# Scatters of a routed kernel issued one at a time behind attention steps, and one key stage moved ahead

## The chip, the cores and the metric

The kernel runs on one core of a Trainium2 chip. The metric is the device time of one execution in microseconds (us). The kernel before takes 1244.17 us as the median of 3 runs (1242.67 to 1245.28). The profiled execution is a run of its own and took 1242.59 us, with a span of 1240.8 us between the first and last instruction.

## The reference

Three layers are computed in float32, one after the other, over 4608 tokens of 512 values.

```python
q_s = np.exp(q - q.max(-1)); q_s /= q_s.sum(-1)          # (8 batches, 8 heads, 576, 64)
k_s = np.exp(k - k.max(2));  k_s /= k_s.sum(2)
x = q_s @ (k_s^T @ v)                                    # then (4608, 512)
e = argmax(x @ w_gate + modality_bias[modality_id])      # one of 8 experts per token
x = gate * (relu(x @ w1[e]) @ w2[e])
out = (((x @ m1) * (x @ m2)) @ w3) @ w_out
```

## The kernel before, in words

**Stages.** An opening of some 180 us computes the attention and the routing. Then come the expert slots (each one expert with up to 512 tokens that were sorted to it), and then the last layer's products. TensorE is fed in float32 pieces: each factor is split into a high and a low part, and three products are summed.

**The opening.** The 8 batches are worked in four pairs, c = 0 to 3. `keys(c)` (L292 on) takes the maximum of the keys over the sequence (VectorE, L302 to L305, `tr`, `mx`), turns it with TensorE (L311, L314, L319), copies the maximum to `kr` (ScalarE, L322), subtracts it on GpSimd in 12 pieces (L328; for c = 0 on VectorE) and takes the exponential on ScalarE (L329) in four pieces. The keys sit in `kt`, two buffers for four pairs: pairs 0 and 2 in `kt0`, pairs 1 and 3 in `kt1`. `kvs(c)` (L332 on) multiplies keys and values (L347, four groups of 72 short matmuls), normalises (L354 to L356) and makes the small matrices `bd` (L360, L363, L368, L371). `queries(n)` (L382, L383) prepares three columns of queries in `qs`. `attend(c, j)`, nine times per pair and here called a step and written (c, j), turns the queries (L397), takes the exponential (L400, `qT`), multiplies with `bd` (L410, 32 short matmuls), reads the result out (ScalarE L420 and L421, VectorE L422 and L423 into a row of `xt`), and after every second step SP stores the rows to `x_dram` (L427). `route(c)` (L436 on) finds each token's expert and its place in the sorted order (VectorE, with one exponential at L453 and a few matmuls at L461, L463). `scatters(c)` (L475) then issues nine indirect DMAs on GpSimd's queue, one for 128 tokens each (L434), which write a token's number and gate, 8 bytes, to its place in `order_dram`. Ahead of each but the first stands a small memset of `nop` (L433).

**What sets the order.** Nothing is issued in program order. `Plan` records each operation with its engine, an assumed cost, the keys that it reads and writes, and a priority; `order()` then lists them, taking on each engine the ready operation with the smallest number (place in the program plus priority). Each engine runs its own list in that order, and waits are on semaphores. A scatter has priority +120, so that it stands behind what is recorded up to 120 places after it.

**After the opening.** `early_table()` (called for c = 2) makes a table of the first expert slots from the counts of pairs 0 and 1. For slot 0 SP reads the table (L608), loads the expert's first weights (`w1r`, L644, 2 MB), and then the token list `ord` (L637), which waits for the 18 scatters of pairs 0 and 1. GpSimd gathers the tokens (L655, four indirect DMAs). ScalarE casts `w1r` (L623, eight pieces) and scales the tokens (L659); VectorE and GpSimd take the low parts (L625); TensorE turns the tokens (L675); ScalarE and VectorE split them (L679, L680); then TensorE runs the first layer (L692) and the second (L712). The buffers of the expert stage are handed over from those of the attention at "Mb", after the last step.

The main loop of the opening is this:

```python
    for c in range(4):
        load("k", c + 2)
        keys(c + 1)
        if c:
            route(c - 1)
            if c < 3:
                scatters(c - 1)
        ...
        for j in range(NT):
            attend(c, j)
            if j % 3 == 2:
                queries(3 * c + j // 3 + 2)
        load("q", c + 2)
        kvs(c + 1)
        load("v", c + 2)
```

Of the kernel before, what the change touches and what calls it, by code (L numbers as in the profile page):

```python
# [21 lines left out]
NT = 9  # L22
# [10 lines left out]
BT = 768  # L33
HB = BT // 2
PAIRS = ((0, 0), (0, 1), (1, 0))
WHY = "the tables hold counts of the 4608 tokens only"


# [81 lines left out]
def K(*a):  # L120
    return a
# [21 lines left out]
def body(tc, q, k, v, mod, wgate, mbias, w1, w2, m1, m2, w3, wo, out):  # L143
    nc = tc.nc
    V, G, SC, PE, SP = nc.vector, nc.gpsimd, nc.scalar, nc.tensor, nc.sync
    P = Plan()
# [116 lines left out]
    def load(n, c):  # L263

        if c >= 4:
            return
        src, t = dict(k=(k, kt), q=(q, qt), v=(v, vt))[n]
        z = c % 2
        for i in range(2):
            dst = t[z][:, 4 * i : 4 * i + 4].rearrange("p g j d -> p g (j d)")  # L270
            fn = lambda dst=dst, i=i: SP.dma_start(dst, src[2 * c + i].rearrange("(g y) (r j) d -> (y r) g (j d)", y=2, j=NT))
            P.add("D", 3.7, fn, w=[K(n, z, g) for g in (2 * i, 2 * i + 1)], slack=1.0)
# [100 lines left out]
    def queries(n):  # L373

        if n >= 12:
            return
        c, g = n // 3, n % 3
        z = c % 2
        q_, x = qt[z], qx[z]
        kq = [K("q", z, g) for g in range(4)]  # L380
        js = slice(3 * g, 3 * g + 3)
        P.add("V", vt_(1536), lambda: V.tensor_reduce(x[:, :, js], q_[:, :, js], axis=AX.X, op=ALU.max), r=kq, w=[K("qx", z, g)])  # L382
        P.add("V", vt_(1536), lambda: V.tensor_tensor(qs[(3 * c + g) % 2].rearrange("p j h d -> p h j d"), q_[:, :, js], x[:, :, js].unsqueeze(3).to_broadcast([128, H, 3, D]), op=ALU.subtract), r=kq + [K("qx", z, g)], w=[K("qs", (3 * c + g) % 2)])  # L383
# [47 lines left out]
    def scatter(dst, src):  # L431
        if scattered[0]:
            G.memset(nop, 0.0)  # L433
        i = G.indirect_dma_start(out=order_dram, out_offset=bass.IndirectOffsetOnAxis(ap=dst, axis=0), in_=src, in_offset=None).ins  # L434
        tc.declare_no_dep(i, group="order", reason="every token has a row of its own")
        tc.add_to_no_dep_group("order", i)  # L436
        scattered[0] = True
# [34 lines left out]
        vv(lambda: V.tensor_scalar(s, s, 1e-9, None, op0=ALU.add), w=["s"])  # L472
        vv(lambda: V.reciprocal(tid[:, c, :, 1].bitcast(F32), s), r=["s"], w=[K("gate", c)])

    def scatters(c, after=()):  # L475
        for t in range(NT):
            P.add("G", (1.3, 0.1), lambda t=t: scatter(pi_[c % 2][:, t : t + 1], tid[:, c, t]), r=[K("pi", c % 2), K("gate", c), "order", *after], w=[K("scat", NT * c + t)], pri=120)


    tab = const.tile([1, 4, X0 + NX], I32, name="tab")  # L480
# [306 lines left out]
    biases()  # L787
    for c in range(4):
        load("k", c + 2)
        keys(c + 1)  # L790
        if c:
            route(c - 1)
            if c < 3:
                scatters(c - 1)
        if 2 * c == BEARLY:
            tpri[0] = -150
            early_table()
        if c == 3:
            fa_keys = [k_ for k_ in P.last if isinstance(k_, tuple) and k_[0] in ("k", "v") and k_[1] == 0] + ["mods", K("mods", 0), K("mods", 1), K("bias", 1), "bs", "bsb", "mod", "modf", "zer"]
            P.add("X", 0.0, to_experts_a, w=fa_keys + ["Ma"])  # L800
        for j in range(NT):
            attend(c, j)
            if j % 3 == 2:
                queries(3 * c + j // 3 + 2)
        load("q", c + 2)
        kvs(c + 1)
        load("v", c + 2)
    fb_keys = [k_ for k_ in P.last if isinstance(k_, tuple) and (k_[0] in ("q", "qs", "qx", "qT", "bd", "bdg", "mx", "kr", "cm", "rk", "kT", "vp") or k_[0] in ("k", "v") and k_[1] == 1)]
    P.add("X", 0.0, to_experts_b, w=fb_keys + ["tr4", "wg", "Mb"] + [K("bk", i) for i in (0, 1, 2, 3, 6, 7)])
# [346 lines left out]
```

## Time and profile before

| | us |
|---|---|
| median of 3 runs | 1244.17 |
| lowest and highest | 1242.67, 1245.28 |
| the profiled execution, its own time | 1242.59 |
| its span | 1240.8 |
| TensorE busy | 1147.5 (92%) |
| VectorE busy | 738.3 (59%) |
| ScalarE busy | 488.5 (39%) |
| GpSimd busy | 442.6 (36%) |

PE is TensorE's matmuls, PEld its weight loads, DVE is VectorE, ACT ScalarE, POOL GpSimd, SP the queue that issues most DMAs. A row of the timeline gives the start, the duration, the engine, the line, the operation, and in brackets the idle time before it and what ended it. "issue" is time in which the engine waited for nothing that the profile shows.

### The profile page before, as it was taken

The numbers are of one execution on the slowest core, as the hardware profiler recorded it, in microseconds if no ns is written. First come the engines' busy times: TensorE is split into PE (matmuls) and PEld (weight loads), VectorE is DVE, ScalarE is ACT, GpSimd is POOL, SyncE is SP. The second block draws the span as 40 slices with busy tenths as digits, with TensorE's granted clock in tenths as the row PEclk, the third lists the DMA queues.
The fourth block names the chain that finished last, engine by engine and source line by source line (L and its number), as shares of the span: only waits on it lengthen the run. The fifth ranks groups of instructions, "written<-read, shape, count | busy, mean of one in ns | idle before, by whom it ended". The sixth has DMA issues, their size and how long they took to land.

```text
span 1240.8 us, 20445 instructions
## 1 busy us (share of the span) xinstructions
PE 1147.5 (92%) x7939; PEld 1010.7 (81%) x7939; DVE 738.3 (59%) x1253; ACT 488.5 (39%) x907; POOL 442.6 (36%) x414
## 2 busy tenths in 40 slices
PE   4777559999989999999999999999999999999996
PEld 3565437888878888888987999999999998888885
DVE  7977678789258878778674745546473555213110
ACT  3544355445335444443463342324232434233220
POOL 0445638545033334323161434333343332111111
PEclk9867779999999999999999999999999999999998
DMA  9971166765236555445664222213131326534211
GB/s 354 391 296 62 61 226 149 272 203 167 81 117 209 162 188 189 164 165 179 222 191 131 86 77 103 79 74 103 51 103 56 139 86 244 197 111 171 101 44 41
DMA packets 84076, 187.52 MB, mean 151 GB/s; under 512 B 13022, under 2 KB 19714, under 8 KB 83970
## 3 DMA queue, kind: packets, MB, share of 16 engines
q1 hardware_dynamic: 76898, 166.68, 39.5%
q0 software_dynamic: 7072, 19.44, 4.6%
q8 instruction: 64, 1.05, 0.4%
q14 instruction: 42, 0.34, 0.1%
HBM read 142.25 MB, written 60.67 MB: 164 GB/s over the span
## 4 chain that ended last, share of the span: by engine, by line
PE 68%; DVE 2%; issue 1%; ACT 0%; DMA 0%; POOLq 0%; ACTq 0%; DVEq 0%
PE pb L1038 28%; PE pb L1114 15%; PE pb L712 12%; PE pb L692 10%; PE pb L931 2%; DVE ar L965 2%; PE pb L675 1%; PE pb L918 0%; DMA out_dram<-ca,oall 0%; DVE tt L907 0%; DVE al L907 0%; POOLq L1152 0%; ACT al L906 0%; DVE thm L907 0%; DVE ca L1014 0%
## 5 line engine op out<-in xcount | busy, mean ns | idle before, releaser
L1038 PE MATMUL pb<-al,ar 128*128 128x384 f32 x1728 | 307.8, 335 | 1.1 <-ACT sx L1044 0.8
L1038 PEld LDWEIGHTS pb<-al,ar 128*128 128x128 f32 x1728 | 300.0, 188 | 1.6 <-ACT sx L1044 1.1
L712 PE MATMUL pb<-ar 128*128 128x512 f32 (+1 forms) x960 | 214.1, 381 | 0.0
L692 PE MATMUL pb<-ar 128*128 128x512 f32 (+1 forms) x960 | 211.4, 380 | 0.0
L692 PEld LDWEIGHTS pb<-ar 128*128 128x128 f32 x960 | 173.6, 189 | 33.9 <-DVE ar L680 0.4
L712 PEld LDWEIGHTS pb<-ar 128*128 128x128 f32 x960 | 173.0, 189 | 32.9
L1114 PE MATMUL pb<-ar 128*128 128x512 f32 x864 | 196.0, 389 | 0.0
L1114 PEld LDWEIGHTS pb<-ar 128*128 128x128 f32 x864 | 162.2, 188 | 33.6
L907 DVE TENSOR_TENSOR ar<-ca,ar 128x512 fp32r<-128x512 f32 x80 | 54.9, 707 | 111.3 <-ACT ar L906 111.2
L1119 POOL DMA_INDIRECT out_dram<-ca,oall x36 | 35.6, 990 | 162.0 <-ACT ca L1117 139.2
L696 ACT ACTIVATE ar<-pb 128x512 fp32r<-128x512 f32 (+1 forms) x80 | 46.2, 578 | 117.9 <-PE pb L692 117.8
L1044 ACT COPY sx<-pb 128x384 f32<-128x384 f32 x96 | 46.1, 481 | 98.8 <-PE pb L1038 98.6
L742 POOL TENSOR_TENSOR ca<-ca 128x512 f32<-128x512 f32 x40 | 55.4, 1391 | 77.8 <-DVE ca L741 74.6
L697 DVE SCALAR_TENSOR_TENSOR ar<-pb,ar 128x512 fp32r<-128x512 f32 (+1 forms) x80 | 52.4, 656 | 42.9 <-ACT ar L696 40.6
L1117 ACT COPY ca<-pb 128x512 f32<-128x512 f32 x36 | 21.1, 585 | 131.2 <-PE pb L1114 101.3
L328 POOL TENSOR_TENSOR kt<-kt,kr 128x384 f32<-128x384 f32 x36 | 45.2, 1291 | 72.1 <-ACT kr L322 60.4
L625 DVE TENSOR_TENSOR ar<-w2r,ar 128x512 fp32r<-128x512 f32 x60 | 46.2, 796 | 37.6 <-ACT ar L623 36.6
L1047 POOL TENSOR_TENSOR ca<-ca,sx 128x384 f32<-128x384 f32 x24 | 27.0, 1124 | 113.9 <-ACT sx L1044 113.9
L1047 POOL TENSOR_TENSOR sx<-sx 128x384 f32<-128x384 f32 x24 | 28.7, 1195 | 104.9 <-ACT sx L1044 104.9
L715 ACT COPY yo<-pb 128x512 f32<-128x512 f32 (+1 forms) x40 | 22.6, 565 | 108.6 <-PE pb L712 96.9
L625 POOL TENSOR_TENSOR ar<-w2r,ar 128x512 fp32r<-128x512 f32 x20 | 31.1, 1554 | 85.7 <-ACT ar L623 85.7
L1044 ACT COPY ca<-pb 128x384 f32<-128x384 f32 x48 | 23.0, 479 | 92.2 <-PE pb L1038 82.6
(248 smaller groups left out, 1675.8 us busy)
## 6 DMA issues: line engine op xcount, KB each, us to landing
w1r<-in_moe_w_dram SPq DMA_DIRECT2D x10, 2048.0 KB
w2r<-in_moe_w_dram SPq DMA_DIRECT2D x10, 2048.0 KB
p_dram<-ca SPq DMA_DIRECT2D x48, 384.0 KB
ca<-p_dram SPq DMA_DIRECT2D x18, 1024.0 KB
ca<-in_moe_w_dram SPq DMA_DIRECT2D x32, 512.0 KB
kt<-in_k_dram SPq DMA_DIRECT2D x8, 1152.0 KB
qt<-in_q_dram SPq DMA_DIRECT2D x8, 1152.0 KB
vt<-in_v_dram SPq DMA_DIRECT2D x8, 1152.0 KB
```

What stands on the lines that cost most here:

```text
L328: P.add(en, c_ / 3 + 0.05, lambda hs=hs, e_=e_, js=js: e_.tensor_tensor(k_[:, hs, js], k_[:, hs, js], r_[:, hs].unsqueeze(2).to_broadcast( ...
L625: P.add(g, c, lambda: e.tensor_tensor(lo(), raw(), hi().bitcast(F32), op=ALU.subtract), r=[K(nm + "r", i), K(nm + "h", i), extra], w=[K(nm ...
L692: PE.matmul(p(), lhsT=W1(i)[:, TURN[kk], ms], rhs=XT(z)[:, kk, cols], start=(kk == 0 and c == 0), stop=(kk == 3 and c == 2))
L696: P.add("S", ps_(N), lambda hh=hh, p=p: SC.activation(hh(), p(), AF.Relu), r=[K("bk", pb), "Mb"], w=[K("hh", h, m) for h in hs])
L697: P.add("V", vt_(N), lambda hh=hh, hl=hl, p=p: V.scalar_tensor_tensor(out=hl(), in0=p(), scalar=0.0, in1=hh().bitcast(F32), op0=ALU.max, o ...
L712: PE.matmul(p(), lhsT=W2(i)[:, f, ns], rhs=HT(y)[:, f, cols], start=(f == 0 and c == 0), stop=(f == 7 and c == 2))
L742: P.add("G", gt_(512), lambda: G.tensor_tensor(Tf, Tf, Qf, op=ALU.add), r=[K("Q", b)], w=[K("T", b)])
L907: P.add("V", vt_(n), lambda: V.tensor_tensor(lo(), src, hi().bitcast(F32), op=ALU.subtract), r=list(sk) + [hk], w=[lk])
L1038: PE.matmul(bk(j), lhsT=Mt[:, f, a, i, m, t], rhs=X(y, x)[:, t], start=(fresh and t == 0 and n == 0), stop=(t == 1 and n == 2), skip_group ...
L1044: P.add("S", ps_(HB), lambda j=j, to=to: SC.copy(S(to), bk(j)), r=[bkk(j)], w=[sk(to)])
L1047: P.add("G", gt_(HB), lambda: G.tensor_tensor(S(1), S(1), S(2), op=ALU.add), r=[sk(2)], w=[sk(1)])
L1114: PE.matmul(bank[z], lhsT=PB(u % 2, i, f)[:, ts], rhs=WP(y, f), start=(f == 0 and n == 0), stop=(f == 7 and n == 2))
```

## The change

The two calls of `scatters` for pairs 0 and 1 become a list, `drops`. A scatter is taken from the list and recorded behind a step, and now reads that step's row of `xt` too; its priority is -900 instead of +120. Of the 18, four stand behind steps (1, 5) to (1, 8), nine behind (2, 0) to (2, 8), two behind a preparation of queries (after (2, 5) and (2, 8)), two behind the two halves of `bd` for pair 3, and one behind (3, 0). The scatters of pairs 2 and 3 stay as they were. `keys(3)` is recorded after step (1, 4); before, it was recorded at the start of c = 2. Lines up to 475 move down by one, those of the expert slots by ten.

```diff
+DROP = ((1, 5), (1, 6), (1, 7), (1, 8), (2, 0), (2, 1), (2, 2), (2, 3), (2, 4), (2, 5), (2, 6), (2, 7), (2, 8), (3, 0))
...
-    def scatters(c, after=()):
-        for t in range(NT):
-            P.add("G", (1.3, 0.1), lambda t=t: scatter(pi_[c % 2][:, t : t + 1], tid[:, c, t]), r=[K("pi", c % 2), K("gate", c), "order", *after], w=[K("scat", NT * c + t)], pri=120)
+    def scatters(c, after=(), ts=range(NT), pri=120):
+        for t in ts:
+            P.add("G", (1.3, 0.1), lambda t=t: scatter(pi_[c % 2][:, t : t + 1], tid[:, c, t]), r=[K("pi", c % 2), K("gate", c), "order", *after], w=[K("scat", NT * c + t)], pri=pri)
+
+    drops = []
+
+    def drip(*keys):
+
+        for key in keys:
+            if drops:
+                c, t = drops.pop(0)
+                scatters(c, [key], [t], -900)
...
     for c in range(4):
         load("k", c + 2)
-        keys(c + 1)
+        if c < 2:
+            keys(c + 1)
         if c:
             route(c - 1)
             if c < 3:
-                scatters(c - 1)
+                drops.extend((c - 1, t) for t in range(NT))
...
         for j in range(NT):
             attend(c, j)
+            if (c, j) == (1, 4):
+                keys(3)
+            if (c, j) in DROP:
+                drip(K("xt", (j // 2 + 5 * c) % 5, j % 2))
             if j % 3 == 2:
                 queries(3 * c + j // 3 + 2)
+                if (c, j) in ((2, 5), (2, 8)):
+                    drip(K("qs", (3 * c + j // 3 + 2) % 2))
         load("q", c + 2)
         kvs(c + 1)
+        if c == 2:
+            drip(*[K("bd", 2 + y) for y in range(2)])
         load("v", c + 2)
```

The planner turns this into other lists. First, GpSimd, from the subtraction of pair 2's keys (`kt_119`) on. `pi_106` holds the places of pair 0's tokens, `pi_107` those of pair 1; `kt_120` are pair 3's keys. Before, at the end of the first run of nine scatters:

```order
L434 DMA order_dram<-tid,pi_106 37376x2
L433 MEMSET nop 128x1
L434 DMA order_dram<-tid,pi_106 37376x2
L328 TENSOR_TENSOR kt_120<-kt_120,kr_147 128x2x192 x12
L433 MEMSET nop 128x1
L434 DMA order_dram<-tid,pi_107 37376x2
```

The same place in the change, from pair 2's subtraction on:

```order
L329 TENSOR_TENSOR kt_119<-kt_119,kr_146 128x2x192 x12
L435 DMA order_dram<-tid,pi_106 37376x2
L434 MEMSET nop 128x1
L435 DMA order_dram<-tid,pi_106 37376x2
L434 MEMSET nop 128x1
L435 DMA order_dram<-tid,pi_106 37376x2
L329 TENSOR_TENSOR kt_120<-kt_120,kr_147 128x2x192
L434 MEMSET nop 128x1
L435 DMA order_dram<-tid,pi_106 37376x2
L329 TENSOR_TENSOR kt_120<-kt_120,kr_147 128x2x192 x11
L434 MEMSET nop 128x1
L435 DMA order_dram<-tid,pi_106 37376x2
```

Before, nine scatters stood together ahead of pair 3's subtraction and nine together behind it. Now four stand ahead of its greater part, and the other 14 behind it, each with a wait for its step.

Second, ScalarE where pair 2's steps open: `bd_154` and `bd_155` are the small matrices that those steps read, `pp_82` their first result, `kt_120` pair 3's keys. In the change:

```order
L364 COPY kTs_158<-pb_75 64x512
L330 ACTIVATE kt_120<-kt_120 128x1152
L372 COPY bd_154<-pb_75 128x4x8
L364 COPY kTs_159<-pb_76 64x512
L454 ACTIVATE ca<-ca 128x72
L330 ACTIVATE kt_120<-kt_120 128x1152
L372 COPY bd_155<-pb_76 128x4x8
L330 ACTIVATE kt_120<-kt_120 128x1152
L421 ACTIVATE ca<-pp_82,eps 128x8
```

Before, the exponentials of `kt_120` stood far behind, among pair 2's last steps. Now three of the four stand here, and the read of the first result is behind all of them.

Third, ScalarE at the first expert slot, after the last step: `w1r` are the weights, `ord_94` the gates of slot 0's tokens, L453 (L454) the exponential of pair 3's routing. Before:

```order
L623 CAST ar<-w1r 128x512 x7
L659 ACTIVATE ca<-ca,ord_94 128x512
L623 CAST ar<-w1r 128x512
L659 ACTIVATE ca<-ca,ord_94 128x512 x2
L679 CAST ar<-pb_76 128x2x256
L659 ACTIVATE ca<-ca,ord_94 128x512
L679 CAST ar<-pb_78 128x2x256
L453 ACTIVATE ca<-ca 128x72
L679 CAST ar<-pb_76 128x2x256
```

In the change:

```order
L633 CAST ar<-w1r 128x512 x8
L669 ACTIVATE ca<-ca,ord_94 128x512 x2
L454 ACTIVATE ca<-ca 128x72
L669 ACTIVATE ca<-ca,ord_94 128x512 x2
L689 CAST ar<-pb_76 128x2x256
L689 CAST ar<-pb_78 128x2x256
```

The routing's exponential now stands ahead of two of the four scalings and of all casts of the turned tokens. On SP, the table reads and slot 0's `w1r` load stand between the stores of pair 2's rows now, where they stood behind all of them.

## Rows read from the trace of the kernel before

**Rows 1.** The page: busy time, share of the span and instructions of each engine.

```profile
PE 1147.5 (92%) x7939; PEld 1010.7 (81%) x7939; DVE 738.3 (59%) x1253; ACT 488.5 (39%) x907; POOL 442.6 (36%) x414
```

**Rows 2.** Timeline of PE: first expert matmuls, and the one later gap.

```profile
185.37 22.25 PE L692 MATMUL pb<-ar 128*128 128x512 f32 x93
...
351.49 1.94 PE L675 MATMUL pb<-ident,ca 128*128 128x128 f32 x8 [4.32 <-DVEq L836]
```

**Rows 3.** Windows of 4 us: stretch, length, busy us per engine (instructions), clock, DMA share, GB/s.

```profile
142.00:146.00 4.00, 0.53 (x2) 0.36 (x2) 0.00 (x0) 0.00 (x0) 3.08 (x5) 0.50 0.06 15
```

**Rows 4.** Timeline of PE, 91 to 152 us: start, duration, line.

```profile
91.44 1.25 PE L410 MATMUL pp<-bd,qT 64*64 64x73 f32 x64
...
97.88 1.11 PE L410 MATMUL pp<-bd,qT 64*64 64x73 f32 x38
...
107.03 0.65 PE L360 MATMUL pb<-ident,bd 128*64 128x128 f32 x2
...
128.76 2.37 PE L347 MATMUL pb<-vp,kt 64*64 64x65 f32 x144
...
135.60 1.20 PE L347 MATMUL pb<-vp,kt 64*64 64x65 f32 x44
...
148.31 2.88 PE L347 MATMUL pb<-vp,kt 64*64 64x65 f32 x92 [1.14 <-issue]
```

**Rows 5.** Timeline of POOL, 78 to 146 us.

```profile
78.61 15.70 POOL L328 TENSOR_TENSOR kt<-kt,kr 128x384 f32<-128x384 f32 x12 [18.45 <-ACT kr L322]
94.48 1.40 POOL L434 DMA_INDIRECT order_dram<-tid,pi  x1 [0.17 <-POOL kt L328]
...
105.69 0.96 POOL L434 DMA_INDIRECT order_dram<-tid,pi  x1 [0.19 <-issue]
118.41 14.62 POOL L328 TENSOR_TENSOR kt<-kt,kr 128x384 f32<-128x384 f32 x12 [11.76 <-DVE ca L422]
...
133.20 0.99 POOL L434 DMA_INDIRECT order_dram<-tid,pi  x1
...
144.49 0.97 POOL L434 DMA_INDIRECT order_dram<-tid,pi  x1 [0.19 <-issue]
```

**Rows 6.** DMA queues (packets, MB, share): whole run; then 94-95, 98-99, 168-169 us.

```profile
q8 instruction: 64, 1.05, 0.4%
...
q8 instruction: 1, 0.02, 5.9%
...
q8 instruction: 1, 0.02, 16.9%
...
q8 instruction: 1, 0.02, 5.5%
```

**Rows 7.** Timeline at the gathers: POOL's first, and PE's last piece of pair 3.

```profile
165.40 0.98 POOL L655 DMA_INDIRECT ca<-x_dram,ord  x1 [19.93 <-DMA x_dram<-ca]
...
171.02 0.56 PE L410 MATMUL pp<-bd,qT 64*64 64x73 f32 x9 [1.07 <-issue]
```

**Rows 8.** Timeline, 91 to 157 us: ACT's exponential; ACT, DVE, PE where pairs 2 and 3 open.

```profile
91.85 1.17 ACT L329 ACTIVATE kt<-kt 128x1152 f32<-128x1152 f32 x1
...
114.46 0.28 ACT L420 ACTIVATE ca<-pp,eps 128x8 f32<-128x8 f32 x1 [2.06 <-PE pp L410]
...
151.04 0.16 DVE L354 TENSOR_SCALAR rk<-pb 128x4 f32<-128x4 f32 x1 [11.43 <-PE pb L347]
...
155.68 1.09 PE L410 MATMUL pp<-bd,qT 64*64 64x73 f32 x32
```

**Rows 9.** Timeline after the last step, 172 to 186 us: DVE and ACT.

```profile
172.76 0.69 DVE L423 TENSOR_TENSOR ca<-pp,ca 128x512 f32<-128x512 f32 x1 [0.20 <-DVE ca L422]
...
176.65 1.34 ACT L659 ACTIVATE ca<-ca,ord 128x512 f32<-128x512 f32 x2
...
182.16 0.26 ACT L453 ACTIVATE ca<-ca 128x72 f32<-128x72 f32 x1 [2.12 <-DVE ca L452]
...
182.85 1.28 DVE L680 TENSOR_TENSOR ar<-pb,ar 128x512 fp32r<-128x512 f32 x2
```

## The prediction, made before the change was run

> **What bounds the kernel now.** I read the page, the timeline of TensorE, the windows of the opening, and then the queues. TensorE is busy for 92% of the span [rows 1]. From the first expert matmul at 185.37 us it streams almost without a gap; the one that stands out later (4.32 us, where the program branches) follows TensorE's own work [rows 2]. So the end moves with the start of the expert stage, nearly one for one, and what counts is how soon the opening ends. The reader should see in the windows of the opening a stretch in which VectorE and ScalarE do nothing at all (0.00 busy), TensorE executes 2 matmuls in 4 us, and its granted clock is 0.50 (the 1.2 GHz level) [rows 3]. Only GpSimd is busy there, with scatters.
>
> The timeline shows what TensorE did. Two steps' 64 short matmuls take 1.25 us when nothing disturbs them; two others begin at 97.88 and are over when the next line starts at 107.03, so 9.15 - 1.25 = 7.9 us are lost. Half of pair 3's key products takes 2.37 us; the other half runs 44 matmuls up to 136.80, then six single ones, and resumes at 148.31: 11.5 us less 0.1 for the six, so 11.4 us [rows 4]. Together **19.3 us**. The trace gives "issue" as the cause: no semaphore. The two runs of nine scatters go from 94.48 to 106.65 and from 133.20 to 145.46 [rows 5]. TensorE does not slow down with the first scatter but 4.5 and 3.6 us later, and at both times an instruction packet of its queue is under way: 64 packets hold all of its 15,878 matmuls and loads [rows 1, 6], about 250 each, and the packet at 98 us takes 16.9% of 16 engines for 1 us, so 2.7 us, where the quiet one at 94 us took 5.9%, so 0.94 [rows 6]. I read this as a fetch that meets indirect transfers: TensorE then gets its instructions a few at a time until these are over. In line with that, the matmuls of pair 3's last steps break up from 168 us on, when the gathers run, and a packet falls there too [rows 6, 7].
>
> **The change part by part.**
>
> *The two runs go: -19.3 us.* Nothing is removed in number: 18 scatters of 0.97 us with their 17 memsets, some 1.27 us each from start to start, stay on GpSimd [rows 5]. What goes is the packing. A gain from below is bounded by VectorE's wait behind the second run, 11.43 us [rows 8], from above by the 19.3 us. I take 19.3, since nothing on ScalarE or VectorE was done beside the stalls [rows 3].
>
> *What the single scatters still cost: +7.6 us.* A scatter waits for its step, the step needs TensorE; so when TensorE stalls, no further scatter comes and the stall ends by itself. The time that one scatter is in flight is bounded by its 0.97 us and by 3.8 us: the last of the second run starts at 144.49, and TensorE flows again at 148.31 [rows 4, 5]. A fetch that falls anywhere in this waits half of it, 1.9 us. Nine packets begin between the ones at 98 and 168 us, one per 7.8 us; the stretch with scatters, about 10 us behind (1, 5) and 20 us of pair 2, holds about 4: 4 x 1.9 = 7.6. Bounds: 0 (every fetch finds a gap) and 4 x 3.8 = 15.2.
>
> *`keys(3)` moves: +2.6 us.* Eight VectorE operations, 4 + 8 on TensorE, one copy, 12 subtractions (14.62 us [rows 5]) and four exponentials move ahead; no DMA moves with them, as the loads are recorded where they were. The cost: ScalarE reads the first result of pair 2 behind three of those exponentials, and the last waits for the last subtraction. Earliest time of that read: 94.31 (end of pair 2's subtraction) + 4 scatters x 1.27 + 14.62 + 1.17 for an exponential = 115.2 [rows 5, 8]. Latest, if pair 3's subtraction starts where it did less the first stall, 118.41 - 7.9 = 110.5: 110.5 + 14.62 + 1.17 = 126.3. The return: pair 3 no longer waits for its own keys, only for pair 2's nine steps, at 1.77 us each as in pair 3 ((171.58 - 155.68) / 9 [rows 7, 8]), and for the chain behind the key products, 155.68 - 151.04 = 4.6 us [rows 8]. So pair 3 opens 15.9 + 4.6 = 20.5 us later, at 135.7 to 146.8. The old order without its stalls opens it at 155.68 - 19.3 = 136.4. The bounds are -0.7 and +10.4; I take +2.6, nearer the early end, because the nine scatters that stood before this subtraction are now four and only VectorE's maxima hold it.
>
> *The first expert slot starts later: +1.5 us.* After the last step (end 173.45) VectorE takes low parts and works on pair 3's routing, so ScalarE's exponential comes as late as 182.16 to 182.42. Before, VectorE's low part of the turned tokens began at 182.85 and the first matmul 2.5 us behind it, at 185.37. Now two scalings (1.34) and a cast (by the scalings' 0.67 each, an estimate) stand between: 182.42 + 1.34 + 0.6 = 184.4 in place of 182.85 [rows 2, 9]. Bounds 0 (the cast of pieces hides it) and +3 (both halves are late).
>
> *The gathers come earlier: 0.* They waited for DMA until 165.40 and broke up the last steps [rows 7]; now they can run beside pair 3's first steps and meet a fetch there. Bounds -3.5 and +2. The `w1r` load, 2 MB, crosses pair 2's stores on SP, and slot 1's `w1r` is queued ahead of slot 0's `w2r`; both are wanted well after they land, so 0: what covers them is TensorE's 22.25 us on the first layer [rows 2]; without that cover a 2 MB load would show.
>
> Sum: -19.3 + 7.6 + 2.6 + 1.5 = **-7.6 us**. The profiled execution is 1242.59 and would become 1235.0. The median of the runs stands 1.58 higher, so I predict 1244.17 - 7.6 = **1236.6 us**.
>
> **The rivals.**
>
> *A. The single scatters cost nothing* and the earlier keys help: -19.3 - 0.7 + 1.5 = -18.5, so 1225.7 us. For it: one scatter is on the way for less than half of a fetch's spacing. Against: three fetches of three that met indirect transfers stalled.
>
> *B. The cost is per scatter, not per run.* 19.3 / 18 = 1.07 us each, wherever it stands: then 0 + 2.6 + 1.5, so 1248.3 us, or less where VectorE's own work hides some. For it: TensorE is slow for as long as transfers go on. Against: the first three scatters of each run cost nothing. The Trainium skill, "DMA: Bandwidth & Descriptors", section SWDGE vs HWDGE vs iDMA, says that each DMA engine takes turns between its queues, so a fetch would only wait its turn; by that rule spacing buys nothing and B is the outcome. The 2.7 us of the packet at 98 us agrees with turns; the 7.9 us that TensorE lost does not. The Trainium skill, "Runtime: NRT & Kernel Launch", section Instruction fetch mechanics, says that fetching the next block is mostly hidden; by that the gaps have another cause and B's number holds too. The rows show a gap at each fetch among scatters, so I give it less than the forecast.
>
> *C. The drip closes up into a run again, and it gets slower.* The place: pair 2's second half, where two scatters follow some steps and GpSimd, held up by the subtraction, has steps in arrears. If a fetch meets three scatters in a row, it waits 3.8 + 2 x 1.27 = 6.3 us; four times: 25.4. Sum -19.3 + 25.4 + 2.6 + 1.5 = +10.2, so 1254.4 us. It decides when a fetch costs over (19.3 - 4.1) / 4 = 3.8 us. For it: 14 scatters x 1.27 = 17.8 us in some 20 us of steps. Against: they wait for steps, which stop with TensorE.
>
> **How the numbers follow.** Forecast 50%, with its own range 1229 to 1243; A 20%; B 16%; C 9%; and 5% that the moved work cancels the gain out. A measurement of this kernel can tell 0.2%, 2.5 us, from no change. Faster: 48 of the forecast, 20 of A and 3 of B (most of it hidden) = 71%. Same: 2 of the forecast, 4 of B and the 5 = 11%. Slower: 9 of B and 9 of C = 18%. The range reaches from A's number to B's, 1225 to 1248; it leaves out C and the far sides of A and B.
>
> **What would show it.** Right: between 95 and 160 us no window of 4 us in which VectorE and ScalarE stand at 0.00; TensorE's "issue" gaps under 4 us each; pair 3's first step near 147; the first expert matmul near 178. The read of (2, 0) comes at 115 to 126 us, behind the exponentials; the step on the keys is wrong if it comes earlier, or if pair 3 waits for its keys all the same. B is right if the gaps add up to 15 us or more in small pieces; C if one of them lasts over 5 us beside consecutive scatters. The whole is wrong if the first expert matmul moves and the end doesn't follow.

## The result, and the profile of the changed kernel

The change takes **1257.11 us** (median of 4 runs, 1256.57 to 1257.52) where the kernel before takes 1243.42 in the same series (1241.72 to 1245.28): a ratio of **1.011 [1.009, 1.013]** (in brackets the 95% interval), so 1.1% slower, clear of the noise. The forecast was 1236.6 with a range of 1225 to 1248, so the measured time lies outside it and on the other side. The profiled run of the change took 1256.57 us, 13.98 more than that of the kernel before, with a span of 1254.9.

The page of the change: busy time, share and instructions of each engine, to be laid beside [rows 1].

```profile
PE 1151.0 (92%) x7939; PEld 1014.3 (81%) x7939; DVE 748.9 (60%) x1253; ACT 489.2 (39%) x907; POOL 435.3 (35%) x414
```

The counts are the same; VectorE is busy 10.6 us longer with the same 1253 instructions. The timeline of TensorE in the change (start, duration, line; in brackets the idle time before and what ended it):

```profile
89.90 1.11 PE L398 MATMUL pb<-ident,qs 128*128 128x128 f32 x4 [4.30 <-ACT qT L401]
...
97.33 1.97 PE L398 MATMUL pb<-ident,qs 128*128 128x128 f32 x8 [3.57 <-ACT qT L401]
...
122.51 1.92 PE L361 MATMUL pb<-ident,bd 128*64 128x128 f32 x8 [10.65 <-DVE bd L357]
...
126.99 2.71 PE L411 MATMUL pp<-bd,qT 64*64 64x73 f32 x58
...
133.55 0.50 PE L348 MATMUL pb<-vp,kt 64*64 64x65 f32 x4 [0.94 <-issue]
...
142.15 3.23 PE L348 MATMUL pb<-vp,kt 64*64 64x65 f32 x107 [0.21 <-issue]
...
158.41 0.91 PE L348 MATMUL pb<-vp,kt 64*64 64x65 f32 x18 [3.47 <-issue]
...
167.11 0.74 PE L411 MATMUL pp<-bd,qT 64*64 64x73 f32 x32
...
198.75 23.91 PE L702 MATMUL pb<-ar 128*128 128x512 f32 x96
```

The first expert matmul comes at 198.75 instead of 185.37 [rows 2], 13.4 us later, and the span is 14.1 us longer: the loss is in the opening. Read from the top, it has four places. TensorE waits 4.30 and 3.57 us for ScalarE's `qT`; 10.65 us for VectorE's `bd`; from 129.9 to 142.15 it gets its matmuls a few at a time, as in the stalls of [rows 4]; and up to 158.41 it stands 3.47 us for "issue" again. Pair 3's first step comes at 167.11 instead of 155.68 [rows 8].

Three of them show in windows of 4 us (stretch and length; busy us and instructions of PE, PEld, DVE, ACT, POOL; clock, DMA share, GB/s):

```profile
112.00:116.00 4.00, 0.00 (x0) 0.00 (x0) 4.00 (x1) 2.23 (x3) 4.00 (x5) 0.70 0.00 0
...
132.00:136.00 4.00, 1.50 (x11) 1.26 (x11) 0.00 (x0) 0.00 (x0) 3.43 (x7) 0.50 0.03 1
...
156.00:160.00 4.00, 1.59 (x22) 1.43 (x22) 0.83 (x4) 0.00 (x0) 0.00 (x0) 0.75 0.86 342
```

At 132 us VectorE and ScalarE stand at 0.00 while GpSimd issues scatters, the very picture of [rows 3]. At 112 us it is a new one: TensorE does nothing, and VectorE spends all 4 us in one instruction. Two timelines show what happens there, GpSimd's first, then VectorE's.

```profile
105.60 1.00 POOL L329 TENSOR_TENSOR kt<-kt,kr 128x384 f32<-128x384 f32 x1 [6.29 <-ACT kr L323]
106.79 0.98 POOL L435 DMA_INDIRECT order_dram<-tid,pi  x1 [0.15 <-issue]
107.80 10.54 POOL L329 TENSOR_TENSOR kt<-kt,kr 128x384 f32<-128x384 f32 x11
...
127.92 0.97 POOL L435 DMA_INDIRECT order_dram<-tid,pi  x1 [4.16 <-DVE t_tas L514]
...
139.36 0.97 POOL L435 DMA_INDIRECT order_dram<-tid,pi  x1 [0.19 <-issue]
```

```profile
107.80 11.17 DVE L449 TENSOR_TENSOR ca<-ca 128x576 f32<-128x576 f32 x1
...
165.17 0.75 DVE L449 TENSOR_TENSOR ca<-ca 128x576 f32<-128x576 f32 x1
```

The product of `route` (L449) takes 0.75 us for pair 2 at 165.17 and 11.17 us for pair 1 at 107.80, where it begins with GpSimd's 11 subtractions of `keys(3)` and ends with them. `bd` stands behind it on VectorE. And the scatters that were to come one by one, each behind a step, run ahead of their steps. The four that are keyed to (2, 0) to (2, 3) start from 118.54 to 122.67, before the first matmul of any of these steps (126.81). Then GpSimd waits 4.16 us for VectorE, as the next scatter is the first of pair 1 and needs the places that `route(1)` works out; from 127.92 to 139.36 the other ten start every 1.27 us, ten in a row.

Summed over the brackets of TensorE's timeline from 55 us to the first expert matmul, the idle time (us) by what ended it is this; all other time is "rest". The kernels from the third line on are told of below; the number behind a dash tells the set of runs, each set being one chip.

| kernel | issue | VectorE | ScalarE | rest | first expert matmul | span |
|---|---|---|---|---|---|---|
| before | 20.4 | 13.9 | 11.1 | 84.9 | 185.37 | 1240.8 |
| the change | 19.4 | 20.2 | 17.2 | 87.0 | 198.75 | 1254.9 |
| e2, keys only - 1 | 11.9 | 18.4 | 14.5 | 79.6 | 179.34 | 1242.4 |
| before (b_again) - 2 | 22.8 | 13.0 | 10.6 | 83.0 | 184.44 | 1242.5 |
| the change (a_again) - 2 | 21.6 | 21.9 | 15.7 | 85.6 | 199.76 | 1257.3 |
| e5, old keys, held - 2 | 6.4 | 18.5 | 18.9 | 80.7 | 179.47 | 1243.2 |
| the change (a_third) - 3 | 21.1 | 20.0 | 16.2 | 84.0 | 196.42 | 1253.5 |
| e10, run alone - 3 | 21.3 | 5.8 | 25.8 | 81.1 | 188.97 | 1255.9 |
| before (b_fourth) - 4 | 5.0 | 8.6 | 19.1 | 81.2 | 168.93 | 1231.2 |
| e1, old keys - 4 | 5.7 | 22.5 | 13.2 | 78.5 | 174.77 | 1239.0 |

So the "issue" time that the change was expected to remove is still there (-1.0), and VectorE (+6.3) and ScalarE (+6.1) are waited for longer; with the rest (+2.1) that makes the 13.4.

### The profile page after: what moved, and what is told of

Same layout as the page of the kernel before. It is cut to its first block, busy times and chain, and to the rows that moved or that the text cites. A ratio compares the mean times of both kernels' runs of the same rounds, so it can differ in the third digit from the quotient of the medians.

```text
span 1254.9 us, 20446 instructions
## 1 busy us (share of the span) xinstructions
PE 1151.0 (92%) x7939; PEld 1014.3 (81%) x7939; DVE 748.9 (60%) x1253; ACT 489.2 (39%) x907; POOL 435.3 (35%) x414
## 4 chain that ended last, share of the span: by engine, by line
PE 67%; DVE 2%; issue 1%; ACT 0%; DMA 0%; POOLq 0%; ACTq 0%; DVEq 0%
PE pb L1057 28%; PE pb L1133 15%; PE pb L722 11%; PE pb L702 10%; PE pb L950 2%; DVE ar L984 2%; PE pb L685 1%; PE pb L937 0%; DMA out_dram<-ca,oall 0%; DVE tt L926 0%; DVE al L926 0%; POOLq L1171 0%; ACT al L925 0%; DVE thm L926 0%; DVE ca L1033 0%
## 5 line engine op out<-in xcount | busy, mean ns | idle before, releaser
L1136 ACT COPY ca<-pb 128x512 f32<-128x512 f32 x36 | 21.1, 585 | 132.3 <-PE pb L1133 101.0
L635 DVE TENSOR_TENSOR ar<-w2r,ar 128x512 fp32r<-128x512 f32 x60 | 48.9, 837 | 38.9 <-ACT ar L633 35.7
```

The costliest lines, as they stand in the source:

```text
L635: P.add(g, c, lambda: e.tensor_tensor(lo(), raw(), hi().bitcast(F32), op=ALU.subtract), r=[K(nm + "r", i), K(nm + "h", i), extra], w=[K(nm ...
```

## The experiments

Five sets were run, each on one chip with runs of the kernel before between them. Ratios are compared between sets, times only within one; where a time of one set is held against another's all the same, the text says so. Edits are shown against the changed kernel, unless it is said otherwise, and cut with "...".

**The kernels again.** The kernel before, unedited, was profiled beside the others in three sets, the change in three. The kernel before: 0.9995 [0.998, 1.001], 1.001 [1.000, 1.003] and, in set 4, 1.000 [0.998, 1.002]. The change: 1.0077 [1.005, 1.010], 1.0065 [1.005, 1.008] and, in set 5, 1.0088 [1.007, 1.011]. The sign of the result stands in four series. The surprise is set 4:

> The kernel before once more, beside the two that follow, so that its profile and theirs are of one chip. Every theory: ratio 1.000, first expert matmul at 184 to 186 us, TensorE's issue idle between 90 and 170 us 16 to 19 us.

The ratio came out as expected, the rest did not. The kernel before took 1232.1 us there (1226 to 1238, 23 runs), as in set 1 (1230.5), against 1243 to 1247 in the other sets. Timeline of its TensorE in set 4, then of GpSimd, then the instruction queue (packets, MB, share) in the windows 102 to 103 and 132 to 133 us:

```profile
100.32 1.49 PE L410 MATMUL pp<-bd,qT 64*64 64x73 f32 x62
102.10 0.30 PE L410 MATMUL pp<-bd,qT 64*64 64x73 f32 x2 [0.29 <-issue]
...
131.19 2.37 PE L347 MATMUL pb<-vp,kt 64*64 64x65 f32 x144
...
168.93 12.63 PE L692 MATMUL pb<-ar 128*128 128x512 f32 x48
```

```profile
96.13 1.15 POOL L434 DMA_INDIRECT order_dram<-tid,pi  x1 [0.18 <-POOL kt L328]
...
106.59 0.97 POOL L434 DMA_INDIRECT order_dram<-tid,pi  x1 [0.19 <-issue]
...
128.89 0.99 POOL L434 DMA_INDIRECT order_dram<-tid,pi  x1 [0.15 <-DVE t_taS L496]
...
139.58 1.12 POOL L434 DMA_INDIRECT order_dram<-tid,pi  x1 [0.19 <-issue]
```

```profile
q8 instruction: 1, 0.02, 10.7%
...
q8 instruction: 1, 0.02, 20.4%
```

Both runs of nine are there, at the same 1.27 us each, and a packet of the instruction queue falls into each; the second takes 20.4% of 16 engines for 1 us, more than the 16.9% of [rows 6]. Yet TensorE loses 0.7 us to "issue" between 90 and 170 us, against 16.6 in the profile of the prediction and 17.5 and 18.9 in sets 2 and 3. So a run of nine scatters and a fetch among them do not make a stall by themselves; the difference goes with the set (all 23 runs of the kernel before in set 4 lie below 1238 us, all of set 5 above 1242). Each set being one chip, the chip is the first suspect, but no view shows what decides it. Against the profile of the prediction, from another series, the first expert matmul comes 16.4 us earlier and the span is 9.6 us shorter: that is the nearest there is to what the stalls cost the kernel before.

**e1: the keys in their old place** (sets 1 and 4). What is left of the change is the single scatters.

```diff
-        if c < 2:
-            keys(c + 1)
+        keys(c + 1)
...
-            if (c, j) == (1, 4):
-                keys(3)
```

> The change with keys(3) recorded at the start of c = 2 again, as before; the scatters stay in the new list. Theory: two losses of the change hang on the early keys, VectorE's product held for 11.17 us at 107.80 while GpSimd subtracts, and the key products of pair 2 that stand behind the keys' work on TensorE; without them the time falls back by 10 to 15 us, to 1242 to 1247 us, and no VectorE instruction of the opening is longer than 3 us. Rival (the loose scatters are the whole loss): 1254 to 1258 us.

> The change with keys(3) put back to its old place (scatters one by one, not held by their steps), a second time, since its first profile had the stalls gone (issue idle 3.1 us between 90 and 170 us, first expert matmul 175.50) and yet 1.0064 of the kernel before. Theory M (the start gained is lost again in the first expert slots, whatever the chip, because VectorE has no idle time there): first expert matmul 6 to 10 us earlier than the kernel before has it on this chip, ratio 0.998 to 1.008, slot 1's first layer within 3 us of the kernel before, and VectorE busy for over 90% between 195 and 215 us. Rival (the first set's chip was one on which the kernel before has no stalls): the start is still 6 to 10 us earlier here, but the ratio falls to 0.990 to 0.996.

Measured: 1.0064 [1.004, 1.009] and 1.0059 [1.004, 1.008], 7 to 8 us slower. No VectorE instruction is longer than 3 us in the first set, as expected; in set 4 one is. The second expectation missed on the start: the first expert matmul comes 5.8 us later than in the kernel before on the same chip (174.77 against 168.93), and the span is 7.8 us longer. There is no stall to remove there, and the table shows where the single scatters cost it: VectorE +13.9, ScalarE -5.9, "issue" +0.7, rest -2.7. They stand between the subtractions of `keys(3)`, which now last from 108.17 to 131.98 instead of 114.06 to 128.70. VectorE and TensorE of the second run show a part of the price:

```profile
125.69 0.33 DVE L535 TENSOR_TENSOR t_tags<-t_tag,t_tas 1x24 f32<-1x24 f32 x1
...
126.59 5.43 DVE L535 TENSOR_TENSOR t_tags<-t_tag,t_tadb 1x24 f32<-1x24 f32 x1
131.95 1.74 DVE L384 TENSOR_TENSOR qs<-qt,qx 128x1536 f32<-128x1536 f32 x1
```

```profile
133.84 1.94 PE L398 MATMUL pb<-ident,qs 128*128 128x128 f32 x8 [8.32 <-DVE qs L384]
```

An operation on 24 numbers, 0.33 us just before, takes 5.43 while five subtractions run in a row on GpSimd (127.20 to 131.98); the queries wait behind it and TensorE 8.32 us for them. The table of the first slots (`early_table`) now falls beside the subtractions. But the long operation can't be the whole price. In set 1's profile TensorE waits 5.50 us for the same queries, and VectorE gets in between the five subtractions, which last 1.34 us each there, not 0.96 (GpSimd, then VectorE's product):

```profile
130.92 6.72 POOL L329 TENSOR_TENSOR kt<-kt,kr 128x384 f32<-128x384 f32 x5
```

```profile
132.15 0.73 DVE L449 TENSOR_TENSOR ca<-ca 128x576 f32<-128x576 f32 x1
```

The rest of the price was not taken apart.

**e2: the keys moved, the scatters in runs as before** (set 1).

```diff
-                drops.extend((c - 1, t) for t in range(NT))
+                scatters(c - 1)
```

> The change with the scatters of pairs 0 and 1 in two runs again (the old calls), keys(3) early. Theory: the early keys lose by themselves, so it stays well above the kernel before, 1250 to 1262 us, with both stalls of TensorE beside the runs and a long VectorE product if GpSimd's subtractions stand together beside it. Rival (the loose scatters are the whole loss): 1240 to 1246 us.

Measured 1.0101 [1.008, 1.012], 12.4 us: this move alone costs more than the upper bound of its term (+10.4). VectorE's product is long, as expected (11.70 us); the two stalls are not there (7.4 us of "issue" between 90 and 170 us, no gap over 2.91), so set 1, like set 4, is taken as one without them.

**e3: each scatter held by its step** (set 1; also in e5, e7 and e8). The memset ahead of a scatter becomes a copy of one value per partition out of what the step wrote.

```diff
-    def scatter(dst, src):
-        if scattered[0]:
+    def scatter(dst, src, step=None):
+        if step is not None:
+            G.tensor_copy(nop, step)
+        elif scattered[0]:
```

> The change, but ahead of each of the 18 scatters GpSimd copies one column of the row (or of the tile) of its step to nop instead of the memset, so that it really waits for that step on the chip. Theory: in the change nothing held the scatters, ten of them ran together from 127.92 to 140.33 us and TensorE stood beside them for 12 us; held to their steps they no longer meet one fetch together: 1246 to 1251 us, TensorE's issue gaps under 4 us each between 125 and 160 us, the long VectorE product still there. Rival (each scatter costs TensorE the same wherever it stands): 1255 to 1259 us. Rival (closed-up run all the same): a gap of over 5 us remains.

Measured 1.0174 [1.015, 1.020], no gain over e4, which does not hold them (1.016 in the same set). One gap of over 4 us is left where under 4 was expected: 4.40 us up to 141.93, ahead of the same 18 matmuls as the 3.47 of the change. The built lists say why the copy was needed at all. GpSimd's list in the change, where ten scatters ran together, with each instruction's waits on semaphores:

```
57 L435 DMA order_dram<-tid,pi_106 37376x2
58 L434 MEMSET nop 128x1 [waits Pool_49]
...
65 L435 DMA order_dram<-tid,pi_107 37376x2 [waits DMASW0_49,DVE_49]
...
67 L435 DMA order_dram<-tid,pi_106 37376x2 [waits DMASW1_49]
```

No scatter waits for a step: the waits that stand there are for the places that VectorE writes (DVE), and for a scatter eight before in the list (DMASW). The key that was added tells the planner alone where to put the scatter in the list; a wait on the chip comes from the tiles that an instruction touches, and a scatter touches none of the step's. So where the change is described as giving each scatter "a wait for its step", and as reading the step's row, that holds for the planner only. In e3 the line is `COPY nop<-ca 128x1 [waits DVE_49,Pool_49]`, and the scatters do wait.

**e4: a memset of 0.1 us between the subtractions of `keys(3)`**, to let VectorE in (set 1).

```diff
+ (... op=ALU.subtract), c == 3 and G.memset(nop, 0.0))
```

> The change with a 0.1 us memset of nop behind each of the 12 subtractions of pair 3's keys on GpSimd, nothing else moved. Theory: the product of route(1) on VectorE is held off its second operand's port by subtractions that follow one another without a gap; a gap lets it in after at most one of them: its 11.17 us become under 3 us and the time falls by 7 to 10 us, to 1247 to 1250 us. Rival (it is held by something else, or the gap is too short): 11 us stay and 1257 to 1259 us.

Measured 1.016 [1.013, 1.019]. The hold is still there, up to the last subtraction, on L451 in place of L449:

```profile
109.73 6.47 DVE L451 TENSOR_TENSOR ca<-ca 128x72 f32<-128x72 f32 x1
```

**e5: old keys and held scatters** (sets 2 and 5), the edits of e1 and e3 together.

> keys(3) at the start of c = 2 as before, and each scatter really held to its step by a one-column copy. Theory A: without early keys nothing holds VectorE for long, and where TensorE doesn't stall beside scatters, holding them to their steps gains nothing: within 0.7% of the kernel before (1225 to 1240 us where that takes 1230). Theory B: the stalls are gone with the packing, 1% below the kernel before.

Measured 0.9997 [0.998, 1.001] and, in set 5, 1.0005 [0.999, 1.002]. Here the stalls do go ("issue" 22.8 to 6.4), the first expert matmul comes 5.0 us earlier in set 2, and the end does not move. Whether the hold or the new places in the list removed the stalls is not separated: e1, with these places and no hold, was run only in sets without stalls. VectorE and ScalarE are waited for 5.5 and 8.3 us longer, and slot 1's first layer begins no earlier than before:

```profile
179.47 13.30 PE L704 MATMUL pb<-ar 128*128 128x512 f32 x48
...
235.28 0.93 PE L704 MATMUL pb<-ar 128*128 128x512 f32 x3
```

The kernel before has that row at 234.35 in this set. In e5 every window of 4 us from 196 to 216 us has VectorE at 4.00. That supports a first slot bound by VectorE's low parts; it was not taken apart further.

**e7: held scatters, the subtractions of `keys(3)` on VectorE** (set 2).

```diff
-            en, e_, c_ = ("G", G, gt_(1152)) if c else ("V", V, vt_(1152))
+            en, e_, c_ = ("G", G, gt_(1152)) if c in (1, 2) else ("V", V, vt_(1152))
```

> As the run with the scatters held to their steps (keys(3) early), but pair 3's 12 subtractions are done by VectorE (0.55 us each, 6.6 us in all) and not by GpSimd. Theory: with no subtraction on GpSimd beside it no VectorE instruction of route(1) is longer than 2 us, and the time falls by some 3 us against the held run (its VectorE operation was held for 4.67 us), if VectorE's own 6.6 us lie beside other work; if they do not, it rises by up to 4 us. Rival (VectorE was held by something other than the subtractions): an operation of over 3 us is there still.

Measured 1.0068 [1.005, 1.009]. TensorE's waits for VectorE fall from the change's 21.9 to 4.7 us and no long instruction is left on VectorE; its waits for ScalarE rise from 15.7 to 30.8.

**e8: the order of the kernel before on every engine, scatters held, two a step** (sets 3 and 5), shown against the kernel before and without e3's copy.

```diff
+DROP = {(1, 5): 2, (1, 6): 2, (1, 7): 2, (1, 8): 3, (2, 4): 2, (2, 5): 2, (2, 6): 2, (2, 7): 2, (2, 8): 1}
...
+                scatters(c, [key], [t], 120 if c else -900, step)
...
-                scatters(c - 1)
+                drops.extend((c - 1, t) for t in range(NT))
```

> The order of the kernel before on every engine (keys(3) at the start of c = 2, nine scatters behind pair 2's subtraction and nine behind pair 3's, the loads on SP as before); only, each scatter is held by a one-column copy to its step, two scatters to a step: pair 0's to steps (1, 5) to (1, 8), pair 1's to (2, 4) to (2, 8). Theory: a run that is held to TensorE's own progress cannot starve it for the length of nine scatters; TensorE's issue waits from 90 to 170 us fall from 17.5 us to under 7, the first expert matmul comes 6 to 12 us earlier than in the kernel before on the same chip, and as the slots' own supply takes part of that back (all of 5 us in the held run with keys(3) as before), the end comes 0 to 8 us earlier, ratio 0.993 to 1.000. Rival (the waits only change their name, from issue to VectorE and ScalarE): first expert matmul within 3 us of the kernel before, ratio 0.998 to 1.002.

> The order of the kernel before on every engine, scatters held two a step. Every theory: its order is the old one, so 0.997 to 1.002 in both cases; it is run to see whether its 0.9983 repeats.

Measured 0.9983 [0.997, 1.000] and 0.9972 [0.996, 0.999]. GpSimd in set 3:

```profile
99.08 1.17 POOL L437 DMA_INDIRECT order_dram<-tid,pi  x1 [0.18 <-POOL nop L434]
...
110.64 0.98 POOL L437 DMA_INDIRECT order_dram<-tid,pi  x1 [0.16 <-issue]
```

The first of the nine waits 3.58 us for its step; from then on each step is over when its scatters' turn comes, and so it is throughout the second nine, behind pair 3's subtraction. They go out 1.4 us apart and the stalls stay ("issue" 25.1 in all, and 19.4 between 90 and 170 us where under 7 was expected). A hold spaces nothing where the step is over before its scatter's turn. It is the one version that came out below the kernel before, by 0.2 to 0.3%; its profile does not show from what.

**e10: the 12 subtractions as one run, with a pause ahead of it** (set 3). A scatter that stood behind the first subtraction moves to the end.

```diff
-DROP = ((1, 5), (1, 6), (1, 7), (1, 8), (2, 0), ..., (3, 0))
+DROP = ((1, 5), (1, 6), (1, 7), (2, 0), ..., (3, 0), (3, 1))
```

> The change without the fourth scatter between the first and the second subtraction of pair 3's keys (the list of steps has (3, 1) at its end in place of (1, 8)): the 12 subtractions stand alone, behind some 6 us in which GpSimd waits for the copy of the maximum. Theory L1 (VectorE is shut out when the subtractions follow straight on another GpSimd instruction): route(1)'s product waits for one subtraction at most, under 2 us, and the first expert matmul comes 8 to 11 us earlier than in the change: 1245 to 1250 us where that takes 1257. Theory L2 (any VectorE operation with two operands in SBUF is shut out by subtractions that follow one another): an operation of 5 to 12 us is there again, and the time is within 3 us of the change.

GpSimd and VectorE in e10:

```profile
103.22 12.07 POOL L329 TENSOR_TENSOR kt<-kt,kr 128x384 f32<-128x384 f32 x12 [5.34 <-ACT kr L323]
```

```profile
105.74 1.03 DVE L449 TENSOR_TENSOR ca<-ca 128x576 f32<-128x576 f32 x1
...
110.86 0.71 DVE L451 TENSOR_TENSOR ca<-ca 128x72 f32<-128x72 f32 x1
```

Beside the same twelve subtractions the product takes 1.03 us, against 10.82 in the change of the same set, and the wait for `bd` at L361 is 1.12 us. The 15 scatters behind the subtractions then run together, 1.27 us apart, and the "issue" time stays (21.3). The ratio is 1.0103 [1.008, 1.013] all the same: the first expert matmul comes 7.5 us earlier than in the change (188.97 against 196.42) and the span is 2.4 us longer. Slot 0's gathers stand behind a scatter of pair 2 in GpSimd's list there, and TensorE waits for the tokens:

```profile
174.06 1.37 POOL L435 DMA_INDIRECT order_dram<-tid,pi  x1 [39.67 <-DVE ar L635]
```

```profile
183.58 0.48 PE L685 MATMUL pb<-ident,ca 128*128 128x128 f32 x1 [12.32 <-ACT ca L669]
```

**e12: e10 with the scatters of pairs 2 and 3 recorded behind slot 1** (set 4).

> The kernel with the subtractions of keys(3) as a run of their own, and with the scatters of pairs 2 and 3 recorded behind slot 1, so that GpSimd's list has the gathers of slots 0 and 1 ahead of all scatters of pair 2. Theory L2 (in the run-alone kernel a pair-2 scatter ahead of slot 0's gathers gave back what the shorter VectorE wait had won): the gathers of slot 0 begin 4 us or more earlier than its 175 us, TensorE's wait of 12.3 us for the scaled tokens falls under 6, the first expert matmul comes at 181 to 186 us, and the ratio goes from 1.0103 to 1.002 to 1.006. Rival M (the slots are bound by VectorE's low parts): the first expert matmul comes earlier, but the ratio stays at 1.008 to 1.012.

Measured 1.0129 [1.009, 1.017], with a wait of 12.04 us for the tokens. It decides nothing: one scatter of pair 2 still stands ahead of the gathers in its list (164.84, they follow at 166.39), and the set is one without stalls, so e10 is no measure for it.

**a_fifth** was to tell what the change costs where there is no stall:

> The change itself once more. In the set before this one the kernel before ran at 1231 to 1232 us with its two runs of nine scatters and without stalls (issue idle 0.7 us between 90 and 170 us); in three others it ran at 1243 to 1249 us with stalls of 17 to 19 us. Theory (the change's added VectorE and ScalarE waits are its own, and the stalls are not decided by the packing): if the kernel before runs at 1230 to 1234 us here, ratio 1.012 to 1.022; if at 1242 to 1250 us, 1.006 to 1.013. Rival (the change carries one cost, whatever the stalls): the ratio stays at 1.006 to 1.013 in both cases.

The kernel before took 1246.9 us in that set, so it could not; e4, the change but for its memsets, in set 1, is the nearest: +1.6%. The profile of a_fifth shows something else. The product began 0.9 us ahead of the 11 subtractions and took 0.75 us, and the hold fell on a later operation, behind `bd`:

```profile
111.56 5.43 DVE L451 TENSOR_TENSOR ca<-ca 128x72 f32<-128x72 f32 x1
```

TensorE waited 1.07 us for `bd`, not 10.65, and this run, 1252.57 us, was the lowest of its six (the others 1255.2 to 1258.6). In e3 and e4 too the hold is on that operation in the profile, and the profiled run is the lowest of four, by 3.5 and 6.5 us. So the same program can come out either way, and what the hold costs depends on where it falls; the runs without a profile can't be told apart.

## Why the prediction was wrong

**"The two runs go: -19.3."** The size was read about rightly for the start: without the stalls the kernel before reaches its first expert matmul 16.4 us earlier (two series compared). Two things failed. First, the step "a scatter waits for its step, ... so when TensorE stalls, no further scatter comes and the stall ends by itself": it took the key in the diff for a wait on the chip. The scatters waited for nothing in the step, ran ahead of it, and ten of them went out together once pair 1's places were there. TensorE got through 38 matmuls from 129.91 to 142.15, which is 0.6 us of work at the 2.37 for 144 of [rows 4]: 11.6 us lost, and in all 19.4 us of "issue" against 20.4. Second, the packing was taken for the whole cause from three coincidences in one profile; set 4 has the packing and the fetches and no stall. Where the scatters did wait, and stood apart in the list, on chips with stalls (e5), these went; where they waited and stood together (e8), they stayed.

**"What the single scatters still cost: +7.6."** e1 measures 7.3 and 7.9 us, so the number is right, but by luck: "issue" in set 4 is 5.7 against 5.0. The cost is in TensorE's waits for VectorE (+13.9), for the queries above all, while the subtractions beside the scatters run in pieces; the prediction charged the move to the queues and never to VectorE.

**"`keys(3)` moves: +2.6", bounds -0.7 and +10.4.** e2 gives +12.4. The prediction timed GpSimd, ScalarE and TensorE, and put what the subtractions would meet on VectorE in their new place at nothing, without a reason. VectorE's product of pair 1's routing met the subtractions and took 11.17 us, and `bd` and so pair 2 waited 10.65 for it. The hold repeats in each profile of the change (10.74 and 10.82 on L449; 5.43 on L451 in set 5) and is gone in e7 (no subtraction on GpSimd) and in e10, so that it comes from the subtractions is shown. What it costs in the end is not: e7 and e10 remove it and stay slower than the kernel before, as other waits grow. The second part is that pair 2's key products stand behind `keys(3)` on TensorE: they start at 104.81. In the kernel before, TensorE did them while it had no `qT` (TensorE, then ScalarE, of the kernel before; last ScalarE of the change):

```profile
86.25 4.25 PE L347 MATMUL pb<-vp,kt 64*64 64x65 f32 x144 [0.95 <-ACT kt L329]
...
95.56 1.73 PE L347 MATMUL pb<-vp,kt 64*64 64x65 f32 x72 [1.07 <-ACT kt L329]
```

```profile
88.61 1.11 ACT L400 ACTIVATE qT<-pb 128x512 f32<-128x512 f32 x2
```

```profile
89.22 1.11 ACT L401 ACTIVATE qT<-pb 128x512 f32<-128x512 f32 x2
```

So ScalarE's `qT` is hardly later in the change (0.6 us, as all work there is by then); TensorE waits 4.30 and 3.57 us for it because the work that filled this time is gone to another place. No run moves the key products alone, so this part is read from the rows and not tested. The read of (2, 0) comes at 129.96, outside the 115 to 126 that was forecast, and pair 3's first step at 167.11 instead of 147. The Trainium skill, "SBUF — State Buffer", section Who interferes with whom, states that a VectorE instruction with two inputs in SBUF contends with a GpSimd one that reads SBUF, and that the order of issue decides which of them blocks. The trace agrees on who is held (L449, L451, L535, all with two such inputs), and e10's 1.03 us fits a wait for one subtraction at most; the 11.17 us are a wait for eleven, which the rule does not state. The prediction should have weighed that section and did not.

**The gathers and the loads: 0.** The gathers did not come earlier: they start 8.05 us before the last read ends in both kernels (165.40 and 173.45; 177.46 and 185.51). The loads are half wrong. Slot 0's 2 MB load moved among pair 2's stores, and a packet of the instruction queue falls beside it (156 to 157 us): 3.47 us of "issue" up to 158.41, with a DMA share of 0.86 in the window. The change shows the same gap in sets 2, 3 and 5. That the load is the cause is read from the rows, not tested.

**"The first expert slot starts later: +1.5."** Right. From the end of the last read to the first expert matmul it was 11.92 us (173.45 to 185.37) and is 13.24 (185.51 to 198.75), +1.3, and by the mechanism given. VectorE's last read, ScalarE, and VectorE's low part in the change:

```profile
184.82 0.69 DVE L424 TENSOR_TENSOR ca<-pp,ca 128x512 f32<-128x512 f32 x1 [0.20 <-DVE ca L423]
```

```profile
194.22 0.26 ACT L454 ACTIVATE ca<-ca 128x72 f32<-128x72 f32 x1 [4.78 <-DVE ca L453]
194.40 1.32 ACT L669 ACTIVATE ca<-ca,ord 128x512 f32<-128x512 f32 x2
195.62 1.05 ACT L689 CAST ar<-pb 128x512 fp32r<-128x512 f32 x2
```

```profile
196.21 1.29 DVE L690 TENSOR_TENSOR ar<-pb,ar 128x512 fp32r<-128x512 f32 x2 [0.89 <-ACT ar L689]
```

**"The end moves with the start of the expert stage, nearly one for one."** It held for the change (+13.4 and +14.1). It did not for an earlier start: e5 -5.0 and +0.7 of the span; e10 against the change -7.5 and +2.4; the kernel before in set 4, against the one of the prediction from another series, -16.4 and -9.6. In these three an earlier start was worth 0.6 of itself at most, and nothing where the first slot's own supply was late.

**The rivals.** B's sign came near (13.0 us of "issue" in pieces under 4 us between 90 and 170 us, 14.3 to 14.7 in the change's other profiles, where 15 was the mark), but not B's mechanism, since 18 scatters cost 0.7 us in set 4. C named the right kind of failure, a drip that closes up, at +10.2 against +14, the nearest of the numbers; its reason, scatters in arrears of their steps, was not the one here, where they ran ahead. It had 9%, because "they wait for steps" was held against it. The window without VectorE and ScalarE, whose absence was to show the forecast right, is there at 132 us.

Sum by what was measured, with the stalls of the kernel before as they are: TensorE's waits for VectorE +6.3, for ScalarE +6.1, "issue" -1.0, the rest +2.1, together +13.4 before rounding, and +0.7 behind it.

**Open:** what decides, from set to set, whether a fetch among scatters stalls; why VectorE gets in between two subtractions in e10, and in e1 in set 1, and not in the change; what makes e8 gain its 0.2 to 0.3%. Not tried: a kernel with no scatter at all, and e1 or e2 in a set with stalls, which would split the change's loss where it was measured.

## What to carry to other kernels

A key that orders a planner's list is not a wait on the chip: before counting on "one by one", look in the built list for the semaphore, and ask whether what it waits for will be over before its turn comes. When GpSimd work moves, look at what VectorE does in the same stretch, above all at operations with two inputs in SBUF, and take the length of GpSimd's run (11 us here) as the upper bound of what one can cost. A stall seen in one profile should be seen on a second chip before its whole length is booked as a gain, and a gain in an opening should be booked only as far as the next stage can take it.

## What the runs showed of the hardware that was not expected

The same program with the same packing loses 17.5 and 18.9 us to "issue" between 90 and 170 us in profiles on two chips, 16.6 in that of the prediction, and 0.7 on a further chip, where its time is about 1% shorter.

A VectorE instruction that takes 0.1 to 0.8 us elsewhere took 3.15 to 11.70 us beside a run of GpSimd subtractions. In all profiles together, 12 runs of three or more of pair 3's subtractions began within 0.04 us of the end of a GpSimd instruction. Eleven held a VectorE instruction and took 0.96 to 0.97 us a subtraction; the twelfth (e1, set 1) held none and took 1.34. The runs behind a pause of 5 us or more lengthened none by more than 1 us, and took 1.01 to 1.34. So one of the two engines paid, either VectorE with one long wait or GpSimd with slower subtractions. A memset of 0.1 us between the subtractions did not free VectorE (6.47 us in e4).

TensorE stood 3.47 us for "issue" beside a 2 MB load, with a packet of the instruction queue in that time (4.40 us at the same place in e3).
